# Long-run loads, an on-chip permute, four PSUM pairs at the start and weight sums spread over batch 1, in a fused ReLU²-attention and ReGLU kernel

## The chip, the cores and the metric

The kernel runs on one core of a Trainium2 chip. The metric is the device time of one execution in microseconds (us). The profile shows five engines: PE (TensorE; its weight loads are listed as PEld), DVE (VectorE), ACT (ScalarE), POOL (GpSimd) and SP (SyncE). SyncE and GpSimd mostly issue DMAs here.

## The reference, cut to what matters

```python
# q, k, v: (8, 12, 448, 64)   w_gate, w_val: (768, 1536)   w_out: (1536, 768)
scores = q @ k.transpose(0, 1, 3, 2) / sqrt(64)
attn   = maximum(scores, 0) ** 2 / 448
x      = (attn @ v) as rows: (8*448, 768)            # 3584 tokens
out    = (maximum(x @ w_gate, 0) * (x @ w_val)) @ w_out
```

The attention needs Q and K with the head dimension on the partitions, so both must be transposed on the way in. One unit of attention is a *quad*: four heads of one batch, so three quads per batch and 24 in all. From the second pair of batches on, the gate/value product uses a Strassen scheme with seven products in place of eight; it needs sums of weight blocks. The output product uses it for every pair.

## The kernel before: the parts that matter

The kernel records operations, and a small planner in the same file gives each of them a place in its engine's instruction order, from assumed durations. At run time each engine executes its list strictly in that order. An instruction that waits holds up everything behind it on its engine (SyncE's timeline below shows eight stores that go out only at 165.79 us, behind transposes).

TensorE's results go to PSUM, which the kernel divides into banks. Two pairs of banks serve attention, four single banks the feed-forward part:

```python
PAIRS = [0, 2]
SINGLES = [7, 6, 5, 4]
```

Batches 0 and 1 are loaded in long runs and transposed on TensorE. For batches 2 to 7 the load itself interleaves heads (runs of one 64-element row, one descriptor for each: 896 descriptors per DMA), and five crossbar transposes per quad (DMAs that transpose what they move), issued by SyncE, put Q and K into `qkT`:

```python
def load_qk(b, g):                       # branch for b >= 2
    st.raw_buf = Buf(r_raw)              # one buffer only (N_RAW = 1)
    for j in range(2):
        hs = slice(4*g + 2*j, 4*g + 2*j + 2)
        src = lambda x: x[b, hs].rearrange("h (p t) d -> p t h d", t=NT)
        st.qk_ops += [dma_in(lambda j=j: st.raw()[64:128, j], src(k), 896, 0.9, ...),
                      dma_in(lambda j=j: st.raw()[0:64, j],   src(q), 896, 0.9)]

def transpose_dma(b, g):
    def emit():
        nc.sync.dma_start_transpose(out=qkT[:, 0]..., in_=raw[0:64]...)        # Q, one DMA
        for j in range(2):
            for o, t0, t1 in ((0, 0, NC + 1), (1, NC + 1, NT)):
                nc.sync.dma_start_transpose(out=kT[:, o:NT:2], in_=raw[64:128, j, t0:t1]...)  # K, four
    op = Op({"SP": (0.2, 0.2)}, emit, deps=st.qk_ops, alloc=[st.qt_buf], reads=[st.raw_buf])
    op.land = 5.0
```

The weight sums of the gate/value product are twelve VectorE subtractions of 128 x 1536. All of them wait for batch 1's whole gate/value product, because three of them overwrite `wv`:

```python
T_ops = make_T([quads[(1, g)].done for g in range(NQ)] + [o for o, _ in ffn])
```

The loads of `w_out` stand in GpSimd's list behind the quads of batch 2, and so behind the wait for the single raw buffer.

## Time and profile before

463.98 us, the median of 3 runs (463.94 to 465.17). The profiled execution has a span of 464.7 us.

The stages below are cut at the first TensorE matmul of each kind: gate/value product (GV) of batches 0 and 1, output product (OUT) and Strassen gate/value product (ST) of each pair of batches. Attention of later batches runs between those matmuls.

| stage | starts at, us | length, us |
|---|---|---|
| attention of batch 0 | 0 | 43.5 |
| GV, batches 0 and 1 | 43.5 | 87.1 |
| OUT, pair 0 | 130.6 | 52.2 |
| ST, pair 1 | 182.8 | 70.6 |
| OUT, pair 1 | 253.4 | 36.6 |
| ST and OUT, pair 2 | 290.0 | 94.6 |
| ST and OUT, pair 3 (no attention left) | 384.6 | 80.1 |

The table of busy time by stretch, cut at these stages, shows where TensorE is not busy. The columns are the stretch and its length, the busy time of each engine with its instruction count, the granted TensorE clock (1.00 is full), the share of the DMA engines, and GB/s.

```profile
core 0: us, PE busy (x) PEld busy (x) DVE busy (x) ACT busy (x) POOL busy (x), PEclk, DMA share, GB/s
0.00:43.49 43.49, 28.00 (x245) 14.21 (x245) 23.89 (x36) 22.16 (x25) 26.43 (x43) 0.85 1.28 179
43.49:130.59 87.10, 80.61 (x514) 34.37 (x513) 61.66 (x91) 42.78 (x58) 31.79 (x34) 0.96 1.06 106
130.59:182.77 52.18, 42.29 (x248) 19.10 (x247) 35.55 (x63) 24.83 (x35) 19.15 (x20) 0.84 0.83 99
182.77:253.41 70.64, 65.52 (x382) 28.30 (x381) 57.49 (x102) 39.28 (x59) 27.94 (x29) 0.95 0.88 101
253.41:290.03 36.62, 32.14 (x215) 15.99 (x213) 28.89 (x56) 14.65 (x23) 13.15 (x15) 1.00 0.90 116
...
384.63:464.70 80.07, 73.02 (x404) 39.21 (x401) 44.36 (x84) 26.50 (x51) 0.00 (x0) 0.99 0.18 43
```

The pace of batch 0 can be read from ScalarE's timeline: the copy of each finished quad into `xT` (columns: start, duration, engine, line, operation and shape, and in brackets the idle time before it and what ended it).

```profile
21.54 0.91 ACT L508 CAST xT<-ps 128x896 bf16<-128x896 f32 x1 [2.25 <-PE ps L493]
31.84 0.91 ACT L508 CAST xT<-ps 128x896 bf16<-128x896 f32 x1 [2.25 <-PE ps L493]
42.10 0.91 ACT L508 CAST xT<-ps 128x896 bf16<-128x896 f32 x1 [2.25 <-PE ps L493]
```

One quad takes 10.3 us, though no engine has that much work for it. The list of waits (who waited, for whom: total, times, longest) names the two chains of the middle part: GpSimd's raw loads wait for the transposes that still read the only raw buffer, and VectorE waits 10.6 us for a `w_out` load that was issued late for that reason; TensorE waits 5.8 us behind VectorE at the same place.

```profile
POOL raw L288 <- DMA qkT<-raw: 126.7, 19, 16.1
DVE woT L583 <- DMA wo<-in_moe_w_out_dram: 10.6, 1, 10.6
PE ps L544 <- DVE hT L554: 5.8, 1, 5.8
```

SyncE's timeline shows the stores standing behind transposes. The transpose at 159.02 waited for its load, the four after it take 5.35 us to issue, and eight stores go out only then:

```profile
159.02 1.23 SPq L414 DMA_TRANSPOSE qkT<-raw  x1
160.34 5.35 SPq L419 DMA_TRANSPOSE qkT<-raw  x4
165.79 5.32 SPq L717 DMA_DIRECT2D out_dram<-o  x8
```

### The profile page before, as it was taken

How to read it: one execution, taken by the hardware profiler on the slowest of the kernel's cores; microseconds unless marked ns; L12 is line 12 of the kernel's file. 1: busy time of each engine (PE TensorE's matmuls, PEld its weight loads, DVE VectorE, ACT ScalarE, POOL GpSimd, SP SyncE). 2: the span in 40 equal slices, each digit the busy share in tenths (PEclk: the TensorE clock that was granted, in tenths of full speed). 3: DMA queues.
4: the chain of work that ended last, by engine and by line, in shares of the span. 5: the costliest groups of instructions: out<-in, count | busy, mean ns of one | idle time of the engine just before them, and what ended most of it. 6: DMA issues, size and time to landing. Idle time of an engine off the chain costs nothing.

```text
span 464.7 us, 7076 instructions
## 1 busy us (share of the span) xinstructions
PE 415.1 (89%) x2580; PEld 195.2 (42%) x2580; DVE 332.8 (72%) x576; ACT 221.9 (48%) x329; POOL 134.9 (29%) x154
## 2 busy tenths in 40 slices
PE   4768999968988948799999978999999999999994
PEld 2333444423433413244444443444444555555552
DVE  3665877709798833788979967988889686666561
ACT  2564555553574522456555434665654634444221
POOL 7745150605533353145333442253200000000000
PEclk9977999997997968799999999999999999999999
DMA  9999989999857996998669898996721332000144
GB/s 128 196 198 198 151 70 100 108 147 79 82 59 87 122 132 92 128 155 70 74 82 90 85 118 147 167 83 68 72 27 27 76 86 52 1 0 2 34 103 102
DMA packets 138659, 44.13 MB, mean 95 GB/s; under 512 B 103808, under 2 KB 138624, under 8 KB 138624
## 3 DMA queue, kind: packets, MB, share of 16 engines
q0 software_dynamic: 94528, 24.39, 54.5%
q1 hardware_dynamic: 44096, 19.29, 20.9%
q8 instruction: 20, 0.33, 0.3%
q14 instruction: 15, 0.12, 0.1%
HBM read 48.76 MB, written 11.01 MB: 129 GB/s over the span
## 4 chain that ended last, share of the span: by engine, by line
PE 71%; DMA 9%; DVE 7%; SPq 4%; ACT 4%; issue 3%; POOL 1%; DVEq 0%; POOLq 0%; ACTq 0%
PE ps L643 29%; PE ps L744 17%; PE ps L544 8%; PE ps L493 6%; PE ps L451 6%; DMA wo<-in_moe_w_out_dram 4%; SPq L419 3%; DMA out_dram<-o 3%; ACT at L465 3%; PE ps L384 2%; DVE at L467 1%; DMA qkT<-raw 1%; DVE at L470 1%; PE ps L455 1%; PE ps L485 1%
## 5 line engine op out<-in xcount | busy, mean ns | idle before, releaser
L465 ACT ACTIVATE at<-ps 128x896 bf16<-128x896 f32 x117 | 104.4, 918 | 69.2 <-PE ps L451 55.3
L470 DVE TENSOR_TENSOR at<-at 128x896 bf16<-128x896 bf16 x168 | 99.7, 618 | 13.5 <-ACT at L465 13.4
L592 ACT COPY f<-ps 128x448 f32<-128x448 f32 x105 | 55.8, 533 | 66.4 <-PE ps L643 64.5
L288 POOL DMA_DIRECT2D raw<-in_k_dram x36 | 46.2, 1284 | 141.0 <-DMA qkT<-raw 126.7
L467 DVE TENSOR_SCALAR at<-ps 128x896 bf16<-128x896 f32 x51 | 55.3, 1085 | 6.9 <-PE ps L451 6.7
L288 POOL DMA_DIRECT2D raw<-in_q_dram x36 | 59.7, 1662 | 0.3 <-DMA wv<-in_moe_w_val_dram 0.3
L643 PE MATMUL ps<-xT,gvT 128*128 128x448 bf16 x216 | 53.3, 356 | 2.6 <-DVE o L734 2.5
L643 PE MATMUL ps<-sx,wv 128*128 128x448 bf16 x216 | 52.8, 353 | 1.7 <-DVE g L662 1.1
L451 PE MATMUL ps<-qkT 64*128 64x448 bf16 x288 | 45.5, 379 | 9.8 <-ACT at L465 7.1
L643 PE MATMUL ps<-xT,wg 128*128 128x448 bf16 x216 | 52.8, 356 | 0.5 <-DVE g L700 0.5
L288 POOL DMA_DIRECT2D vv<-in_v_dram x44 | 36.4, 1044 | 47.5 <-PE ps L493 40.4
L643 PEld LDWEIGHTS <-gvT 128*128 128x128 bf16 x324 | 31.1, 98 | 37.1 <-issue 9.9
L734 DVE SCALAR_TENSOR_TENSOR o<-ps,f 128x384 f32<-128x384 f32 x40 | 22.0, 554 | 31.1 <-DMA out_dram<-o 16.0
L744 PE MATMUL ps<-wo,hT 128*128 128x384 bf16 x240 | 43.8, 326 | 0.2 <-DVE hT L666 0.2
L744 PEld LDWEIGHTS <-sh 128*128 128x128 bf16 x288 | 27.9, 101 | 36.2 <-issue 10.8
L744 PEld LDWEIGHTS <-hT 128*128 128x128 bf16 x312 | 30.1, 99 | 24.6 <-issue 5.8
L744 PE MATMUL ps<-woT,sh 128*128 128x384 bf16 x144 | 30.1, 359 | 8.4 <-DVE sh L781 8.3
L544 PE MATMUL ps<-xT,wv 128*128 128x448 bf16 x144 | 32.3, 362 | 5.8 <-DVE hT L554 5.8
L493 PE MATMUL ps<-at,vv 128*64 128x448 bf16 x264 | 33.2, 393 | 0.0
L544 PE MATMUL ps<-xT,wg 128*128 128x448 bf16 x144 | 32.6, 364 | 0.0
L594 ACT ACTIVATE f<-ps 128x384 f32<-128x384 f32 x40 | 19.6, 491 | 27.2 <-PE ps L744 26.0
L508 ACT CAST xT<-ps 128x896 bf16<-128x896 f32 x24 | 21.7, 905 | 19.4 <-PE ps L493 19.4
(56 smaller groups left out, 442.1 us busy)
## 6 DMA issues: line engine op xcount, KB each, us to landing
out_dram<-o SPq DMA_DIRECT2D x112, 96.0 KB, 2.9
vv<-in_v_dram POOLq DMA_DIRECT2D x44, 128.0 KB, 5.2
raw<-in_k_dram POOLq DMA_DIRECT2D x36, 112.0 KB, 3.9
raw<-in_q_dram POOLq DMA_DIRECT2D x36, 112.0 KB, 5.0
wg<-in_moe_w_gate_dram POOLq DMA_DIRECT2D x6, 384.0 KB, 11.3
wv<-in_moe_w_val_dram POOLq DMA_DIRECT2D x6, 384.0 KB, 11.2
wo<-in_moe_w_out_dram POOLq DMA_DIRECT2D x4, 576.0 KB, 13.2
qkT<-raw SPq DMA_TRANSPOSE x90, 3.2
```

What stands on the lines that cost most here:

```text
L288: op = Op({"POOL": (0.5 + 0.0004 * n_desc,) * 2}, lambda: nc.gpsimd.dma_start(out=dst(), in_=src), deps=deps, alloc=alloc)
L451: nc.tensor.matmul(ps[:, ps2.idx + h2, :S], lhsT=self.k_of(j, h2, c), rhs=self.q_of(j, h2), start=True, stop=True)
L465: nc.scalar.activation(at_t[at.idx], src, AF.Relu)
L467: nc.vector.tensor_scalar_max(at_t[at.idx], src, 0.0)
L470: sq = Op({"DVE": (0.535, 0.66)}, lambda: nc.vector.tensor_tensor(at_t[at.idx], at_t[at.idx], at_t[at.idx], ALU.mult), deps=[relu])
L493: nc.tensor.matmul(ps[o, ps2.idx + j, :S], lhsT=st.v_of(2 * j + h2, c), rhs=at_t[self.at[NC * j + c].idx][:, h2, :], start=False, stop=(c ...
L508: nc.scalar.copy(dst, src)
L544: nc.tensor.matmul(ps[:, pb.idx, :S], lhsT=w[:, kd, fc], rhs=xT_t[xbuf[b].idx][:, kd, :], start=(kd == 0), stop=(kd == KD - 1))
L592: nc.scalar.copy(dst, src)
L643: nc.tensor.matmul(ps[:, pb.idx, :S], lhsT=w(g)[:, fc], rhs=rhs, start=start and g == 0, stop=stop and g == KH - 1, skip_group_check=True)
L734: op = Op({"DVE": V384}, lambda: nc.vector.scalar_tensor_tensor(o_t[ob.idx], ps[:, pb.idx, :OH], float(out_scale), f_t[fb.idx][:, :OH], AL ...
L744: nc.tensor.matmul(ps[:, pb.idx, :OH], lhsT=lhs(kf), rhs=rhs(kf), start=start and kf == 0, stop=kf == FH - 1, skip_group_check=True)
```

## The change

The intent has several parts in one edit:

1. Q and K of every batch are loaded in long runs (256 descriptors per DMA). VectorE (or ScalarE) then interleaves the slots on the chip, so that each quad needs two crossbar transposes instead of five. The raw buffer is free as soon as the permute is done.
2. Batch 0 may use all four pairs of PSUM banks.
3. Weight sums: nine of the twelve are rewritten so that they no longer need the overwritten block, and can run during batch 1's gate/value product.
4. The planner prices SyncE (2.6 us per quad's transposes, 1.2 us per store), plans VectorE and ScalarE work that follows a load 4 us late, models DMAs differently, and prefers ScalarE by 0.3 us.
5. The `w_out` loads come earlier and batch 1's loads one weight chunk later. One attention buffer and one output buffer are given up for the permute's buffer.
6. Two smaller things stand in the same edit: around batch 0's last quad, the PV product (attention times V) and the next transposes come at other places in the order, and the four sums of `w_out` are rewritten so that the one that overwrites `wo` comes last.

```diff
-    PAIRS = [0, 2]
+    PAIRS, FIRST_PAIRS = [0, 2], [0, 2, 4, 6]
...
+    BIAS = 0.3
+    MARGIN = 4.0
...
+            if e in ("DVE", "ACT"):
+                r = max([r] + [d.end + self.MARGIN for d in op.deps if d.load])
...
-    N_QT, N_AT, N_X, N_F, N_G, N_O = 3, 11, 3, 5, 4, 6
-    N_RAW, N_VV = 1, 3
+    N_QT, N_AT, N_X, N_F, N_G, N_O = 3, 10, 3, 5, 4, 5
+    N_RAW, N_PERM, N_VV = 1, 1, 3
...
+        src = lambda x: x[b, hs].rearrange("h (p t) d -> p h t d", t=NT)
+        k_op = dma_in(lambda: st.raw()[64:128], src(k), 256, 1.15, alloc=[st.raw_buf] if b >= NPE else [])
+        q_op = dma_in(lambda: st.raw()[0:64], src(q), 256, 1.15)
...
+        perm = Op({"DVE": (0.25 + 0.2 * len(runs),) * 2, "ACT": (2.1, 2.2)}, None, deps=st.qk_ops, alloc=[pb], reads=[st.raw_buf])
+            for o, t0, t1 in runs:                       # two runs (even batches) or three (odd)
+                dst = perm_t[pb.idx][:, :, o:o + 2 * (t1 - t0) - 1:2]
+                ... tensor_copy(dst, src[:, :, t0:t1])
+            for a in range(2):
+                nc.sync.dma_start_transpose(out=qkT_t[st.qt_buf.idx][:, a]..., in_=perm_t[pb.idx][64 * a:64 * a + 64]...)
-        op = Op({"SP": (0.2, 0.2)}, emit, deps=st.qk_ops, alloc=[st.qt_buf], reads=[st.raw_buf])
-        op.land = 5.0
+        op = Op({"SP": (2.6, 2.6)}, emit, deps=[perm], alloc=[st.qt_buf], reads=[pb])
+        op.land = 2.8
...
-        st = Op({"SP": (0.15, 0.15)}, emit, deps=[op], reads=[ob])
+        st = Op({"SP": (1.2, 1.2)}, emit, deps=[op], reads=[ob])
...
-        if c % 2 == 0:
+        if c % 2 == 1:
             load_qk(1, c // 2)
...
-    T_ops = make_T([quads[(1, g)].done for g in range(NQ)] + [o for o, _ in ffn])
+    T_ops = make_T([quads[(1, g)].done for g in range(NQ)], [o for o, _ in ffn])   # second list: only for the three sums that overwrite wv
```

More of the change, by code (lines that the diff above doesn't have):

```diff
@@ L56 @@
     SWITCH = 0.1
+    BIAS = 0.3
+    MARGIN = 4.0
+    RESERVE = 0.0
     def __init__(self):
@@ L86, in best @@
                 s = max(r, self.t.get(e, 0.0) + self.SWITCH)
-            if c is None or s + busy < c[0]:
-                c = (s + busy, s, e)
+            f = s + busy + (self.BIAS if e == "DVE" and len(op.engs) > 1 else 0.0)
+            if c is None or f < c[0]:
+                c = (f, s, e)
         return c[1], c[2], r
@@ L98, in commit @@
         if op.load:
-            self.dmaq = max(self.dmaq, s + occ + 1.0) + op.load
-            op.end = self.dmaq + 1.0
+            self.dmaq = max(self.dmaq, s + occ + 0.3) + op.load
+            op.end = self.dmaq + 2.0
             self.landed.append(op.end)
@@ L185, in plan @@
             left = deadline(sg) - last_burst + 1 if sg is not None and deadline(sg) is not None else 0
-            gap = left_work[sg] / max(1, left) if left > 0 else 0.0
+            gap = max(0.0, left_work[sg] - P.RESERVE) / max(1, left) if left > 0 else 0.0
         else:
@@ L247 @@
     woT = pool.tile([128, 3, FH, OH], BF16, name="woT")
-    raw_t = [pool.tile([128, 2, NT, 2, D], BF16, name=f"raw{i}") for i in range(N_RAW)]
+    raw_t = [pool.tile([128, 4, NT, D], BF16, name=f"raw{i}") for i in range(N_RAW)]
+    perm_t = [pool.tile([128, 2, NT, 2, D], BF16, name=f"perm{i}") for i in range(N_PERM)]
     vv_t = [pool.tile([128, 4, NC + 2, D], BF16, name=f"vv{i}") for i in range(N_VV)]
@@ L260 @@
     r_ps = Res(8)
-    r_raw, r_vv, r_qt, r_at = Res(N_RAW), Res(N_VV), Res(N_QT), Res(N_AT)
+    r_raw, r_perm, r_vv, r_qt, r_at = Res(N_RAW), Res(N_PERM), Res(N_VV), Res(N_QT), Res(N_AT)
     r_x, r_f, r_g, r_o = Res(N_X), Res(N_F), Res(N_G), Res(N_O)
@@ L323, with slot_order, main_slot @@
     SIG = [x for c in range(NC) for x in (c, NC + 1 + c)] + [NC]
-    def q_slots(b):
-        if b < NPE:
-            return SIG if b % 2 == 0 else SIG[-1:] + SIG[:-1]
-        return list(range(NT))
-    def q_main(b):
-        return 0 if b % 2 == 0 else 1
-    def k_main(b):
-        return 1 if b < NPE and b % 2 else 0
+    def slot_order(b):
+        return SIG if b % 2 == 0 else SIG[-1:] + SIG[:-1]
+    def main_slot(b):
+        return b % 2
     def load_qk(b, g):
         st = quads[(b, g)] = Quad()
-        if b < NPE:
-            hs = slice(4 * g, 4 * g + 4)
-            st.raw_buf = None
-            st.raw = lambda: early_raw(b, g)
-            src = lambda x: x[b, hs].rearrange("h (p t) d -> p h t d", t=NT)
-            k_op = dma_in(lambda: st.raw()[64:128], src(k), 256, 1.2)
-            q_op = dma_in(lambda: st.raw()[0:64], src(q), 256, 1.2)
-            st.qk_ops = [k_op, q_op]
-        else:
-            st.raw_buf = Buf(r_raw)
-            st.raw = lambda: raw_t[st.raw_buf.idx]
-            st.qk_ops = []
-            for j in range(2):
-                hs = slice(4 * g + 2 * j, 4 * g + 2 * j + 2)
-                src = lambda x: x[b, hs].rearrange("h (p t) d -> p t h d", t=NT)
-                st.qk_ops += [dma_in(lambda j=j: st.raw()[64:128, j], src(k), 896, 0.9,
-                                     alloc=[st.raw_buf] if j == 0 else []),
-                              dma_in(lambda j=j: st.raw()[0:64, j], src(q), 896, 0.9)]
+        hs = slice(4 * g, 4 * g + 4)
+        st.raw_buf = None if b < NPE else Buf(r_raw)
+        st.raw = lambda: early_raw(b, g) if b < NPE else raw_t[st.raw_buf.idx]
+        src = lambda x: x[b, hs].rearrange("h (p t) d -> p h t d", t=NT)
+        k_op = dma_in(lambda: st.raw()[64:128], src(k), 256, 1.15, alloc=[st.raw_buf] if b >= NPE else [])
+        q_op = dma_in(lambda: st.raw()[0:64], src(q), 256, 1.15)
+        st.qk_ops = [k_op, q_op]
     def load_v(b, g):
@@ L368, in load_v @@
         st.v_of = lambda hh, c: st.vv()[:, hh, 1 + c, :]
-        v0 = dma_in(lambda: st.vv()[0:64, :, 1:NC + 2], src[:, :, 0:NC + 1], 256, 0.7,
+        v0 = dma_in(lambda: st.vv()[0:64, :, 1:NC + 2], src[:, :, 0:NC + 1], 256, 0.66,
                     alloc=[st.vv_buf] if st.vv_buf else [])
-        v1 = dma_in(lambda: st.vv()[64:128, :, 0:NC + 1], src[:, :, NC:NT], 256, 0.7)
+        v1 = dma_in(lambda: st.vv()[64:128, :, 0:NC + 1], src[:, :, NC:NT], 256, 0.66)
         st.v_ops = [v0, v1]
@@ L376, in transpose_pe @@
         st = quads[(b, g)]
-        ps2 = bank2()
+        ps2 = bank2(FIRST_PAIRS if b == 0 else PAIRS)
         def emit():
@@ L381, in emit @@
             for j in range(2):
-                for i, t in enumerate(q_slots(b)):
+                for i, t in enumerate(slot_order(b)):
                     for h2 in range(2):
@@ L410, in transpose_dma, with emit_perm @@
         st.qt_buf = Buf(r_qt)
-        def emit():
-            raw, qkT = st.raw(), qkT_t[st.qt_buf.idx]
-            nc.sync.dma_start_transpose(out=qkT[:, 0].rearrange("p j (t c) -> p (j t) c", c=P2),
-                                        in_=raw[0:64].rearrange("p j t h d -> p (j t h d)"))
-            for j in range(2):
-                kT = qkT[:, 1, j].rearrange("p (t c) -> p t c", c=P2)
-                for o, t0, t1 in ((0, 0, NC + 1), (1, NC + 1, NT)):
-                    nc.sync.dma_start_transpose(out=kT[:, o:NT:2], in_=raw[64:128, j, t0:t1].rearrange("p t h d -> p (t h d)"))
-        op = Op({"SP": (0.2, 0.2)}, emit, deps=st.qk_ops, alloc=[st.qt_buf], reads=[st.raw_buf])
-        op.land = 5.0
+        pb = Buf(r_perm)
+        m = main_slot(b)
+        runs = [(m, 0, NC + 1 - m), (1 + m, NC + 1, NT)] + ([(0, NC, NC + 1)] if m else [])
+        perm = Op({"DVE": (0.25 + 0.2 * len(runs),) * 2, "ACT": (2.1, 2.2)}, None, deps=st.qk_ops, alloc=[pb], reads=[st.raw_buf])
+        def emit_perm():
+            src = st.raw().rearrange("p (j h) t d -> p j t h d", j=2)
+            for o, t0, t1 in runs:
+                dst = perm_t[pb.idx][:, :, o:o + 2 * (t1 - t0) - 1:2]
+                if perm.eng == "ACT":
+                    nc.scalar.copy(dst, src[:, :, t0:t1])
+                else:
+                    nc.vector.tensor_copy(dst, src[:, :, t0:t1])
+        perm.emit = emit_perm
+        def emit():
+            for a in range(2):
+                nc.sync.dma_start_transpose(out=qkT_t[st.qt_buf.idx][:, a].rearrange("p j (t c) -> p (j t) c", c=P2),
+                                            in_=perm_t[pb.idx][64 * a:64 * a + 64].rearrange("p j t h d -> p (j t h d)"))
+        op = Op({"SP": (2.6, 2.6)}, emit, deps=[perm], alloc=[st.qt_buf], reads=[pb])
+        op.land = 2.8
         st.qt_ops = [op]
-        others.append(op)
+        others.extend([perm, op])
     xop, xbuf = {}, {}
@@ L437, in k_of @@
         def k_of(self, j, h2, c):
-            m = k_main(self.b)
+            m = main_slot(self.b)
             o, n = (P2 * m + 128 * c, 128) if c < NC else (0 if m else 2 * NC * P2, P2)
@@ L442, in s @@
         def s(self, i):
-            ps2 = bank2()
+            ps2 = bank2(FIRST_PAIRS if self.b == 0 else PAIRS)
             tail = i == 2 * NC
@@ L477, in pv @@
             b, g, st = self.b, self.g, self.st
-            ps2 = bank2()
+            ps2 = bank2(FIRST_PAIRS if b == 0 else PAIRS)
             def emit_tail():
@@ L559, in gv_plain, with make_T @@
         last_use[("gv", b)] = ops
-    def make_T(after):
-        res = {}
+    def make_T(after, last):
+        res = []
         for g in range(KH):
-            prev = []
-            for o, a, c in ((lambda g: gvT[:, 1, g], lambda g: wv[:, 2 * g + 1], lambda g: wv[:, 2 * g]),
-                            (lambda g: wv[:, 2 * g], lambda g: wv[:, 2 * g], lambda g: wg[:, 2 * g]),
-                            (lambda g: gvT[:, 0, g], lambda g: wv[:, 2 * g + 1], lambda g: wv[:, 2 * g]),
-                            (lambda g: gvT[:, 2, g], lambda g: wg[:, 2 * g + 1], lambda g: gvT[:, 0, g])):
-                op = Op({"DVE": (0.85, 0.97)}, lambda o=o, a=a, c=c, g=g: nc.vector.tensor_tensor(
-                    o(g), a(g), c(g), ALU.subtract), deps=after + prev)
-                others.append(op)
-                prev = [op]
-            res[g] = prev
-        return [x for p in res.values() for x in p]
+            for o, a, c, f in ((lambda g: gvT[:, 1, g], lambda g: wv[:, 2 * g + 1], lambda g: wv[:, 2 * g], ALU.subtract),
+                               (lambda g: gvT[:, 0, g], lambda g: wg[:, 2 * g], lambda g: gvT[:, 1, g], ALU.add),
+                               (lambda g: gvT[:, 2, g], lambda g: wg[:, 2 * g + 1], lambda g: gvT[:, 0, g], ALU.subtract)):
+                op = Op({"DVE": (0.85, 0.97)}, lambda o=o, a=a, c=c, f=f, g=g: nc.vector.tensor_tensor(o(g), a(g), c(g), f),
+                        deps=after + res[-1:] + list(wg_op.values()) + list(wv_op.values()))
+                others.append(op)
+                res.append(op)
+        for g in range(KH):
+            op = Op({"DVE": (0.85, 0.97)}, lambda g=g: nc.vector.tensor_tensor(wv[:, 2 * g], wv[:, 2 * g], wg[:, 2 * g], ALU.subtract),
+                    deps=res[-1:] + last)
+            others.append(op)
+            res.append(op)
+        return res
@@ L577, in make_To @@
     def make_To():
         res = []
-        for i, (o, a, c) in enumerate(((lambda: woT[:, 1], lambda: wo[:, 1, 1], lambda: wo[:, 0, 1]),
-                                       (lambda: wo[:, 0, 1], lambda: wo[:, 0, 1], lambda: wo[:, 0, 0]),
-                                       (lambda: woT[:, 0], lambda: wo[:, 1, 1], lambda: wo[:, 0, 1]),
-                                       (lambda: woT[:, 2], lambda: wo[:, 1, 0], lambda: woT[:, 0]))):
-            op = Op({"DVE": (1.25, 1.38)}, lambda o=o, a=a, c=c: nc.vector.tensor_tensor(o(), a(), c(), ALU.subtract),
+        for o, a, c, f in ((lambda: woT[:, 1], lambda: wo[:, 1, 1], lambda: wo[:, 0, 1], ALU.subtract),
+                           (lambda: woT[:, 0], lambda: wo[:, 0, 0], lambda: woT[:, 1], ALU.add),
+                           (lambda: woT[:, 2], lambda: wo[:, 1, 0], lambda: woT[:, 0], ALU.subtract),
+                           (lambda: wo[:, 0, 1], lambda: wo[:, 0, 1], lambda: wo[:, 0, 0], ALU.subtract)):
+            op = Op({"DVE": (1.25, 1.38)}, lambda o=o, a=a, c=c, f=f: nc.vector.tensor_tensor(o(), a(), c(), f),
@@ L759, in out_tail @@
         wd = list(wo_op.values())
-        slots = ((b, q_slots(b)[-1]), (b + 1, q_slots(b + 1)[0]))
+        slots = ((b, slot_order(b)[-1]), (b + 1, slot_order(b + 1)[0]))
         a0 = out_mm(lhs(0), w(0, 0), A, True, h_lo + wd, seg, [A], [hb], grp=(pr, "t"))
@@ L790, in out_strassen @@
             A, Dk, E = bank(), bank(), bank()
-            s0, s1 = [tuple((bb, q_slots(bb)[q_main(bb) + 2 * i + z]) for z in range(2)) for bb in (b, b + 1)]
+            s0, s1 = [tuple((bb, slot_order(bb)[main_slot(bb) + 2 * i + z]) for z in range(2)) for bb in (b, b + 1)]
             gr = lambda n: (pr, i, n)
@@ L816 @@
         load_gv(c)
-        if c % 2 == 0:
+        if c % 2 == 1:
             load_qk(1, c // 2)
             load_v(1, c // 2)
-    for g in range(NQ):
-        load_qk(2, g)
-        load_v(2, g)
-        if g > 0:
-            load_out(0, g - 1)
-    load_out(1, 0)
-    load_out(1, 1)
+    load_qk(2, 0)
+    load_v(2, 0)
+    for par in range(2):
+        for hf in range(2):
+            load_out(par, hf)
+        load_qk(2, 1 + par)
+        load_v(2, 1 + par)
     for b in range(3, B):
@@ L856 @@
         att.append((qd.s(2 * NC), burst))
-        PV(n - 1)
-        T(n + 1)
+        if n != NQ:
+            PV(n - 1)
+        if n != NQ - 1:
+            T(n + 1)
         burst += 1
@@ L862 @@
         att += [(qd.s(4), burst), (qd.s(5), burst)]
+        if n == NQ - 1:
+            burst += 1
+            PV(n)
+            T(n + 1)
     burst += 1
```

## The prediction

> **What bounds the kernel.** TensorE is busy 415 of 464.7 us (page, part 1). Busy time times granted clock (table by stretch) gives about 398 us of work, so some 67 us are idle or half-clock time, in three places:
> - Start, 0 to 43.5 us: batch 0's quads come every 10.3 us (timeline: score eviction at 23.50, then 33.77), though ScalarE and VectorE have only about 6.2 us of work per quad. The chain of waits alternates "scores, eviction": two PSUM pairs are too few. TensorE is cold (twelve PV matmuls take 2.45 us, later 1.32).
> - 100 to 110 us: TensorE waits 5.8 us. VectorE stands 10.6 us at the out-weight sum for a w_out load that GpSimd issued only at 85 us, because the single raw buffer waits for the transposes (126.7 us in the list of waits).
> - 130 to 200 us: twelve gate/value weight sums (0.95 us each) in a clump, then stores queued behind five crossbar DMAs per quad (1.24 us of SyncE each) that wait for loads: stores ready near 160 issue at 165.8, output buffers return late, TensorE idles 11.2 us in 160 to 200 at clock 0.79.
>
> From 200 to 250 TensorE is 99% busy, VectorE 87%; after 385 only TensorE work is left.
>
> **What the change does.**
> - Batch 0 may use four PSUM pairs. I take 7 to 7.5 us per quad (engine sums above; a cold quad of TensorE is 8.1). Gate matmuls start near 32 instead of 43.5: −11 us. Weight loads (198 GB/s there) still arrive ahead of use, by my count of bytes.
> - Raw loads of batches 2 to 7: 36+36 DMAs of 896 descriptors become 18+18 of 256; GpSimd issue falls from 1.3/1.7 to about 0.65 us each (the early loads' time), software-queue packets from 94.5k to about 39k. By itself off the critical path. The Trainium skill ("DMA: Bandwidth & Descriptors", Specifications) says transfers below 512 B do a read-modify-write; this trace shows only 103.8k packets below 512 B.
> - Transposes 90 → 36: SyncE per quad 6.6 → 2.5 us; the raw buffer is free after the permute; the w_out loads move forward. The 100–110 stall goes: −6.5 us with its clock.
> - The plan now prices SyncE, so stores no longer hide behind transposes.
> - Added: 18 permutes, all on VectorE (instruction order), 45 copies; estimate 0.7 us per quad if they run at four elements per cycle (skill, "VectorE: DVE Perf Modes", Mode 4×_2P; this trace has no such instruction), 1.1 at the squares' rate: +12 to 19 us of VectorE. 13 relus move to ScalarE: −14.
> - 130–189: my sum is TensorE 41, VectorE about 40 us; I expect 45 instead of 59: −14.
> - 250–300, 4.6 us idle: about −3. Last 80 us unchanged (both orders end with 252+150 matmuls).
>
> Sum: about 464 − 36 = 428 us.
>
> **In the profile after:** batch 0 pitch near 7.5 us; first gate matmul near 32; no wait for w_out; transposes start within a microsecond of the permute; no raw-load waits on transposes; TensorE clock near 1.0 from 50 on (skill, "TensorE: Matmul & The Clock Gate", Part 1: an idle window of about 3.4 us halves it; this trace agrees, matmuls after the 6.5 us gap at 171 take about double); VectorE share 77–80%.
>
> **What would make it wrong:** permutes near 1.5 us, or standing in VectorE's in-order queue for loads; VectorE the new bound through 110–200 (then 440); five output buffers too few; batch 0 still DMA-limited. If all gaps close: 415.
>
> 428 us, range 416 to 442; faster 0.95, same 0.04, slower 0.01.

## More of the kernel before

Timings come from three sittings. The first gave the result (before and after). Sitting A ran four experiments (a1, b1, c1, d1) on one chip. Sitting B ran the other eight on another chip, with the changed kernel repeated among them. Each sitting timed the kernel before too.

In OUT of pair 0, TensorE is idle for 10 of 52 us and has 0.84 of its clock while it works.

## The result, and the profile after

430.22 us, the median of 4 runs (428.66 to 430.43), against 463.96 us for the kernel before in the same rounds (with a fourth run of it). The ratio is 0.926, with a 95% interval of 0.923 to 0.929. Ratios in this document are the mean time of one kernel's fast runs over that of the other's of the same rounds, so they are not quite the ratio of the quoted medians. The prediction, 428 us with a range of 416 to 442, holds. Its parts do not all hold.

The same table of busy time by stretch, for the changed kernel, cut at its own stages:

```profile
0.00:29.49 29.49, 17.84 (x208) 9.57 (x209) 18.60 (x29) 19.37 (x23) 19.71 (x34) 1.00 1.24 174
29.49:120.62 91.13, 83.86 (x551) 36.13 (x548) 67.72 (x109) 53.03 (x72) 25.07 (x38) 0.94 1.13 143
120.62:156.03 35.41, 35.41 (x249) 16.93 (x247) 33.02 (x66) 23.33 (x34) 6.12 (x10) 1.00 0.89 162
156.03:222.84 66.81, 64.56 (x390) 28.42 (x389) 58.38 (x113) 44.21 (x67) 11.12 (x19) 1.00 0.76 94
222.84:253.61 30.77, 30.63 (x208) 16.01 (x206) 23.13 (x51) 15.15 (x24) 4.92 (x8) 1.00 0.72 129
...
349.08:428.60 79.52, 73.01 (x403) 39.21 (x401) 44.35 (x84) 26.53 (x51) 0.00 (x0) 0.98 0.18 43
```

| stage | before, us | after, us | difference | my prediction |
|---|---|---|---|---|
| attention of batch 0 | 43.5 | 29.5 | −14.0 | −11 |
| GV, batches 0 and 1 | 87.1 | 91.1 | +4.0 | −6.5 |
| OUT pair 0, ST and OUT pair 1 | 159.4 | 133.0 | −26.4 | −17 (14 + 3) |
| ST and OUT, pair 2 | 94.6 | 95.5 | +0.9 | 0 |
| last pair | 80.1 | 79.5 | −0.6 | 0 |
| sum | 464.7 | 428.6 | −36.1 | −34.5 named |

Three of the rows are off by 3 to 10.5 us each, and the errors cancel. A part of the first two is work that changed sides: 37 of TensorE's matmuls, 28 of them the transposes of one quad (1.71 us at 41.85 us in the kernel before), stand in front of the first gate matmul before and behind it after. Together these two rows gave −10.0 us, where I had −17.5. (The attention work is spread a little differently over the stages. The instruction order has 36 of the large score matmuls in OUT of pair 0 in both kernels, but 60 instead of 52 in the stage after it and 12 instead of 20 in the next, which is why those three stages are summed.)

The start: ScalarE's copies of the three quads are now 6 us apart, not 10.3.

```profile
16.83 0.96 ACT L511 CAST xT<-ps 128x896 bf16<-128x896 f32 x1
22.94 0.91 ACT L511 CAST xT<-ps 128x896 bf16<-128x896 f32 x1 [0.28 <-PE ps L496]
28.81 0.91 ACT L511 CAST xT<-ps 128x896 bf16<-128x896 f32 x1 [3.33 <-PE ps L496]
```

The list of waits: the 126.7 us of raw-load waits on transposes are gone, and so is the wait for `w_out`. GpSimd now waits 18.6 us for permutes. There is a new line for VectorE: it waits for the transposes to let go of the only permute buffer, and TensorE waits for VectorE's evictions of scores.

```profile
POOL raw L295 <- DVE perm L415: 18.6, 4, 9.4
DVE perm L415 <- DMA qkT<-perm: 5.2, 2, 4.7
PE ps L454 <- DVE at L470: 4.5, 4, 2.0
```

The timeline shows that new stall; with the half clock after it, it is the larger part of what keeps the GV stage long. A smaller wait comes first: TensorE stands 2.65 us until 37.76 us for the Q load of batch 1's second quad, which part 5 of the change had put one weight chunk later (f2 below removes it). VectorE's second permute stood 4.65 us, until the first transposes had landed. TensorE ran out of score evictions twice, 1.58 and 2.04 us, and then worked at about half speed until 85 us.

```profile
37.76 0.97 PE L375 MATMUL ps<-ident,gvT 128*64 128x128 bf16 x28 [2.65 <-DMA gvT<-in_q_dram]
...
69.78 0.69 DVE L415 COPY perm<-raw 128x1024 bf16<-128x1024 bf16 x2 [4.65 <-DMA qkT<-perm]
...
72.06 0.55 PE L454 MATMUL ps<-qkT 64*128 64x448 bf16 x4 [1.58 <-DVE at L470]
...
74.66 0.56 PE L454 MATMUL ps<-qkT 64*128 64x448 bf16 x2 [2.04 <-DVE at L470]
```

SyncE's timeline in OUT of pair 0: two transposes per quad, and no store stands behind a long row of them.

```profile
144.12 3.64 SPq L421 DMA_TRANSPOSE qkT<-perm  x2
147.85 7.85 SPq L722 DMA_DIRECT2D out_dram<-o  x10
155.81 3.30 SPq L421 DMA_TRANSPOSE qkT<-perm  x2
```

The permutes themselves came out as estimated. The groups by shape (count, busy us, mean ns, idle before them) sum to 14.7 us for 18 quads, 0.8 us per quad; without shapes, overlaps counted once, they are 13.2 us, 0.73 per quad.

```profile
L415 DVE COPY perm<-raw 128x768 bf16<-128x768 bf16 x27 | 8.9, 357 | 0.5 <-DMA qkT<-perm 0.5
L415 DVE COPY perm<-raw 128x1024 bf16<-128x1024 bf16 x9 | 3.8, 417 | 4.7 <-DMA qkT<-perm 4.7
L415 DVE COPY perm<-raw 128x256 bf16<-128x256 bf16 x9 | 2.0, 226 | 0.0
```

From 256 to 768 elements the copy grows by 131 ns, which is 3.9 elements per ns. That agrees with the mode of four elements per cycle in the Trainium skill ("VectorE: DVE Perf Modes", Mode 4×_2P; the page's clock is 0.96 GHz).

### The profile page after: what moved, and what is told of

It is laid out like the page before. It is cut to its first block, busy times and chain, and to the rows that moved or that the text cites. A ratio compares the mean times of both kernels' runs of the same rounds, so it can differ in the third digit from the quotient of the medians.

```text
span 428.6 us, 6975 instructions
## 1 busy us (share of the span) xinstructions
PE 399.1 (93%) x2580; PEld 190.3 (44%) x2580; DVE 324.5 (76%) x600; ACT 236.3 (55%) x350; POOL 73.1 (17%) x118
## 3 DMA queue, kind: packets, MB, share of 16 engines
q0 software_dynamic: 38656, 24.39, 43.2%
## 4 chain that ended last, share of the span: by engine, by line
PE 70%; DMA 12%; DVE 11%; issue 2%; ACT 2%; POOL 2%; SPq 1%; DVEq 0%; POOLq 0%
PE ps L648 25%; PE ps L749 22%; PE ps L547 10%; DMA gvT<-in_q_dram 7%; PE ps L496 6%; PE ps L454 5%; DMA qkT<-perm 5%; DVE at L470 2%; DVE at L473 2%; DVE g L667 1%; PE ps L458 1%; DVE perm L415 1%; DVE g L689 1%; PE ps L488 1%; DMA out_dram<-o 1%
## 5 line engine op out<-in xcount | busy, mean ns | idle before, releaser
L468 ACT ACTIVATE at<-ps 128x896 bf16<-128x896 f32 x130 | 114.8, 923 | 49.1 <-PE ps L454 36.3
L295 POOL DMA_DIRECT2D vv<-in_v_dram x44 | 27.2, 628 | 194.5 <-PE ps L496 184.7
L470 DVE TENSOR_SCALAR at<-ps 128x896 bf16<-128x896 f32 x38 | 41.2, 1084 | 15.1 <-PE ps L454 15.0
L454 PE MATMUL ps<-qkT 64*128 64x448 bf16 x288 | 42.5, 365 | 7.9 <-DVE at L470 4.5
L749 PEld LDWEIGHTS <-hT 128*128 128x128 bf16 x312 | 29.5, 98 | 23.5 <-issue 4.2
L496 PE MATMUL ps<-at,vv 128*64 128x448 bf16 x264 | 31.2, 367 | 1.6 <-DVE at L473 1.6
L648 PEld LDWEIGHTS <-wv 128*128 128x128 bf16 x216 | 20.2, 97 | 25.1 <-issue 8.4
L689 DVE CUSTOM_DVE_ANT_0 g<-ps,f 128x448 bf16<-128x448 f32 x36 | 22.3, 620 | 10.7 <-PE ps L648 10.6
L648 PEld LDWEIGHTS <-wg 128*128 128x128 bf16 x216 | 20.4, 98 | 22.1 <-issue 4.2
L599 ACT ACTIVATE f<-ps 128x384 f32<-128x384 f32 x40 | 19.7, 492 | 18.3 <-PE ps L749 16.4
## 6 DMA issues: line engine op xcount, KB each, us to landing
wg<-in_moe_w_gate_dram POOLq DMA_DIRECT2D x6, 384.0 KB, 11.3
```

The costliest lines, as they stand in the source:

```text
L295: op = Op({"POOL": (0.5 + 0.0004 * n_desc,) * 2}, lambda: nc.gpsimd.dma_start(out=dst(), in_=src), deps=deps, alloc=alloc)
L454: nc.tensor.matmul(ps[:, ps2.idx + h2, :S], lhsT=self.k_of(j, h2, c), rhs=self.q_of(j, h2), start=True, stop=True)
L468: nc.scalar.activation(at_t[at.idx], src, AF.Relu)
L470: nc.vector.tensor_scalar_max(at_t[at.idx], src, 0.0)
L496: nc.tensor.matmul(ps[o, ps2.idx + j, :S], lhsT=st.v_of(2 * j + h2, c), rhs=at_t[self.at[NC * j + c].idx][:, h2, :], start=False, stop=(c ...
L648: nc.tensor.matmul(ps[:, pb.idx, :S], lhsT=w(g)[:, fc], rhs=rhs, start=start and g == 0, stop=stop and g == KH - 1, skip_group_check=True)
```

## The experiments

All times are medians; "before" in sitting A was 460.67 us (455.51 to 462.78, seven runs) and in sitting B between 460.99 and 461.55 us as runs were added. The changed kernel was timed again under its own name in sitting B only (but see d1). All kernels but one gave correct results; that one is named.

### a1: the four PSUM pairs alone, in the kernel before

```diff
-    PAIRS = [0, 2]
+    PAIRS, FIRST_PAIRS = [0, 2], [0, 2, 4, 6]        # used by batch 0's transposes, scores and PV
```

> The kernel before with one thing of the change: batch 0 may use four PSUM pairs. In the changed kernel the first gate matmul came at 29.5 us instead of 43.5. Theory (the PSUM pairs alone are the start's gain): first gate matmul near 30 to 31 here too, and 450 to 453 us in all (-11 to -14). Rival (the start's gain needs the other load order or is swallowed later, because the wait for w_out at 100 us and the transposes depend on loads that come no earlier): first gate matmul near 30, but 457 to 463 us in all.

Measured: 459.37 us, ratio 1.000 (0.989 to 1.011): no gain that the runs can tell, though the interval leaves room for 5 us either way. The first gate matmul did come at 31.0 us in place of 43.5. But the GV stage that follows took 95.8 us in place of 87.1, OUT of pair 0 started only 3.8 us earlier than before, and the list of waits has a new line:

```profile
PE ps L451 <- DMA qkT<-raw: 9.0, 1, 9.0
```

TensorE came earlier to the scores of a later quad and waited there for its transposes. VectorE's wait for `w_out` also grew, from 10.6 to 13.9 us. The rival holds: the pairs alone bring the start forward, and the gain is given back at the next thing that depends on the loads.

### b1 and b2: the changed kernel with the old Q and K path

The Q and K path of batches 2 to 7 is put back (896-descriptor loads, no permute, five transposes), with the planner told that five transposes cost 6.6 us of SyncE; everything else of the change stays.

```diff
-        op = Op({"SP": (2.6, 2.6)}, emit, deps=[perm], alloc=[st.qt_buf], reads=[pb])
+        op = Op({"SP": (6.6, 6.6)}, emit, deps=st.qk_ops, alloc=[st.qt_buf], reads=[st.raw_buf])   # five DMAs, from raw
```

> The changed kernel with the Q and K path of the kernel before for batches 2 to 7 (896-descriptor loads, no permute, five crossbar DMAs per quad), everything else kept, the plan told that the five cost 6.6 us of SyncE. Theory (the long-run loads and two-DMA transposes carry the gain in the output stage of pair 0): 440 to 448 us (+10 to +18), the extra in 100 to 200 us, with late stores. Rival (the weight sums' new place and the priced plan carry it; the data path is off the critical path): 428 to 434 us.

b1 gave a wrong result (not-a-number): I had mixed up the row order of odd batches, so some output rows were never stored. Its time was 442.42 us in sitting A (ratio 0.964, 0.955 to 0.972).

> The run b1 repeated with its mistake mended: b1 used the wrong row order for odd batches, so that some output rows were never stored; its stores and its work were the same in number and size. Expected: correct, and the same time within noise, 0.955 to 0.97 of the kernel before.

b2 was correct, 442.18 us in sitting B (ratio 0.959, 0.953 to 0.965), 9.9 us above the changed kernel there. GpSimd's waits for the transposes are back:

```profile
POOL raw L294 <- DMA qkT<-raw: 162.7, 21, 12.8
```

TensorE was busy 23.3 of the 30 us from 130 to 160, at 0.91 of its clock; in the changed kernel it was busy 28.7 of them. So the data path is worth about 10 us when the rest of the change is there.

The loss is not where my theory put it. Against the changed kernel of the same sitting, OUT of pair 0 starts 6.4 us earlier in b2 (115.0 us, 121.4 there) and is short: 33.1 us, with 217 matmuls in it in place of 249, although stores still went out behind rows of five transposes (10 of them at 128.15 us, 14 at 144.00). The Strassen stage after it is the long one: 81.1 us with 434 matmuls, in place of 67.9 us with 390. In it TensorE waits 4.98 us for transposes, and has half its clock for a time after that:

```profile
159.10 0.93 PE L457 MATMUL ps<-qkT 64*128 64x448 bf16 x4 [4.98 <-DMA qkT<-raw]
```

Just as telling is the rest: with the old data path, the other parts together are already at 0.959.

### c1: the weight sums in one clump again

```diff
-    T_ops = make_T([quads[(1, g)].done for g in range(NQ)], [o for o, _ in ffn])
+    T_ops = make_T([quads[(1, g)].done for g in range(NQ)] + [o for o, _ in ffn])   # and the old make_T, make_To
```

> The changed kernel with the weight sums of the kernel before: all twelve gate/value sums after batch 1's gate/value stage, in one clump (nine more VectorE sums of 0.95 us in the output stage of pair 0). Theory (moving the sums is a large part of the 24 us that stage gained): 436 to 442 us (+7 to +12), all of it in 120 to 170 us. Rival (VectorE has room there once SyncE is free): 429 to 432 us.

Measured: 434.73 us (433.86 to 436.62), ratio 0.948 (0.941 to 0.956). The changed kernel was not in this sitting under its own name, but d1 below turned out to run the same instructions in the same order, at 431.69 us on the same chip, which makes the cost about 3 us. OUT of pair 0 took 41.2 us (120.89 to 162.11) in place of 35.4, but the Strassen stage after it was shorter (64.1 in place of 66.8). The clump costs something, less than the 7 to 12 us of the theory and more than the rival's nothing, and part of it is won back one stage later.

### d1: the old prices of SyncE in the planner

```diff
-        op = Op({"SP": (2.6, 2.6)}, ...);  op.land = 2.8;  st = Op({"SP": (1.2, 1.2)}, ...)
+        op = Op({"SP": (0.2, 0.2)}, ...);  op.land = 5.0;  st = Op({"SP": (0.15, 0.15)}, ...)
```

> The changed kernel planned with the old prices of SyncE (0.2 us a quad's transposes, 0.15 us a store, 5 us to land). Only the order of instructions can change. If pricing SyncE matters: 436 to 445 us with stores queued behind transposes. If two transposes per quad that wait on no load make the order harmless: 428 to 432 us.

Measured: 431.69 us (429.72 to 433.2), ratio 0.940 (0.931 to 0.949), the same as the changed kernel's ratio of 0.939 in sitting B. OUT of pair 0 took 35.4 us here as well. The trace says why: on every engine d1 runs the same operations in the same order as the changed kernel (compared by operation, line and tile, over 2,580 matmuls, 600 VectorE, 350 ScalarE and 148 SyncE instructions). The old prices change no place in the plan. So my sentence "the plan now prices SyncE, so stores no longer hide behind transposes" put the credit in the wrong place. Whether another order would do harm, with two transposes per quad, this run does not test. What it gives is the changed kernel once more, in sitting A.

### The changed kernel again, as a yardstick

> The changed kernel unchanged, as the yardstick for the runs beside it on this chip: 0.926 of the kernel before, 427 to 431 us.

Measured: 432.32 us (432.13 to 432.9), ratio 0.939 (0.933 to 0.945), a little above what I had written. On this chip the kernel before ran 1% faster than in the first sitting and the changed kernel did not. Differences below are taken against 432.32.

### a2: the changed kernel with two PSUM pairs

```diff
-    PAIRS, FIRST_PAIRS = [0, 2], [0, 2, 4, 6]
+    PAIRS, FIRST_PAIRS = [0, 2], [0, 2]
```

> The changed kernel without the four PSUM pairs of batch 0. In the kernel before, the four pairs alone brought the first gate matmul forward by 12.5 us, but a new wait of 9 us for a crossbar transpose (80 to 100 us) ate most of it. Theory (the pairs are worth their full 12 to 14 us only once the loads and transposes of batch 2 keep up, as they do here): 440 to 445 us here, first gate matmul near 42. Rival (the start's gain is eaten here too, by the stall at 70 to 80 us, which sits at a fixed time set by the loads): 431 to 436 us.

Measured: 436.28 us (434.24 to 439.86), ratio 0.948 (0.941 to 0.955): +4.0 us. The first gate matmul came at 40.6 us against 31.1, 9.5 us later, but OUT of pair 0 started only 6.9 us later. (Its profiled execution was its slowest, 438.0 us of span, against 430.5 for the changed kernel's in this sitting.) So the rival is nearer: also in the changed kernel a part of the start's gain is given back, in the GV stage.

### e1: the w_out loads late, as before

```diff
-    load_qk(2, 0); load_v(2, 0)
-    for par in range(2):
-        for hf in range(2): load_out(par, hf)
-        load_qk(2, 1 + par); load_v(2, 1 + par)
+    for g in range(NQ):
+        load_qk(2, g); load_v(2, g)
+        if g > 0: load_out(0, g - 1)
+    load_out(1, 0); load_out(1, 1)
```

> The changed kernel with the w_out loads where the kernel before had them, behind batch 2's quads. In the changed kernel the first two transposes were in flight beside two w_out loads and took 11.2 us to land (5.2 in the median); VectorE stood 4.7 us for the permute buffer they held, and TensorE lost 4.4 us and its clock from 70 to 80 us. Theory (contention with the bulk loads makes the transposes slow): first transposes land in under 6 us, no stall at 70, 423 to 427 us. Rival (the landing is slow whatever runs beside it, or the later w_out brings back a wait for it near 100 us): 428 to 433 us.

Measured: 433.14 us (428.36 to 434.37), ratio 0.939 (0.931 to 0.946): no difference. My theory that the `w_out` loads alone make the first transposes slow falls: they still took up to 9.4 us to land, and VectorE still stood 2.8 us. The timeline shows why the edit could not separate the two. The first permute frees the raw buffer. GpSimd then issued the next K and Q loads, two V loads and the first `w_out` load at 61.4 to 63.8 us, and the transposes of the same permute were issued at 61.2. The permute itself releases the traffic that runs beside its own transposes.

That this traffic slows them is not isolated by an experiment. These are the landing times in both kernels (issue to landing, us, lowest/median/highest of 2 to 6 transposes, and the GB/s of the stretch):

| kernel, stretch (us) | GB/s | landing of transposes |
|---|---|---|
| before, 120 to 140 | 74 | 2.3 / 2.4 / 3.4 |
| before, 80 to 105 (`w_out` in flight) | 119 | 9.6 / 11.5 / 13.2 |
| after, 55 to 68 | 168 | 8.1 / 9.7 / 11.2 |
| after, 92 to 105 | 92 | 9.1 / 9.2 / 9.2 |
| after, 200 to 250 | 108 | 3.5 / 3.7 / 5.2 |

The Trainium skill ("DMA: Bandwidth & Descriptors", § Issuing engines are not separate DMA queues) says that DMAs of the scalar, sync and gpsimd engines all run on the same 16 DMA engines and interleave. The mean GB/s of a stretch is a poor guide (see 92 to 105 us), so I took, from the packets in the changed kernel's trace, the share of the 16 DMA engines' time that GpSimd's queue filled while each transpose was in flight. Of the 36 transposes, the 13 that landed within 4.0 us had at most 0.06 of it beside them; the 16 that took 6.4 to 11.2 us had 0.51 to 1.01. That agrees with the page, as a correlation; in the kernel before it is weaker, with landings under 4 us at a share of up to 0.97.

### e2: a second permute buffer for one quad

```diff
-        pb = Buf(r_perm)
+        pb = Buf(r_perm) if (b, g) != (2, 1) else Buf(Res(1))      # that quad's buffer lies in sx, free until pair 1
```

> The changed kernel with a second permute buffer for the second quad of batch 2 (in the space of a tile that is free until pair 1), so that VectorE need not wait at 65 to 70 us for the first transposes to land. The landing itself stays at about 11 us. Theory (VectorE's in-order wait for the one permute buffer, not the late landing, is what stops TensorE from 70 to 80 us): VectorE idle before that permute gone, TensorE busy 9 or more of 10 us in 70 to 80, 422 to 426 us. Rival (the scores of that quad wait for the landing anyway): 427 to 431 us.

Measured: 428.15 us (427.22 to 429.4), ratio 0.930 (0.925 to 0.935), 4.2 us below the changed kernel; the four runs of each do not overlap. VectorE's idle time before the permutes on the old buffer fell from 5.6 to 1.6 us, and TensorE was busy 7.6 of the 10 us from 70 to 80 in place of 6.1, with the clock at 0.83 and then, from 80 on, at 1.00 (0.71 from 80 to 90 in the changed kernel). VectorE's in-order wait for the buffer was the larger part of the stall. What stays (0.8 and 0.5 us waits for ScalarE's evictions near 73 to 75 us) comes from an order that runs two bursts of scores together. TensorE did not reach the nine busy microseconds that I had written.

### g1: every permute executed twice

```diff
-            for o, t0, t1 in runs:
+            for o, t0, t1 in runs + runs:
```

> The changed kernel with every permute executed twice, the plan not told: 0.68 to 0.77 us more of VectorE in each of 18 quads, 13 us in all. If VectorE were the bound of the attention part: +10 to +13 us, 440 to 445. If TensorE is the bound and VectorE has slack (76% busy): +1 to +5 us, 430 to 436.

Measured: 437.09 us (434.39 to 439.69), ratio 0.949 (0.942 to 0.956): +4.8 us for 11.3 us more of VectorE (24.5 in place of 13.2). So a little less than half of an added VectorE microsecond shows in the time: VectorE is neither the bound nor free. (The doubled permute also makes everything that waits for a permute later: GpSimd's waits for permutes are 25.2 us in place of 18.6. The run does not separate the two.)

### k1: the new Q and K path alone, in the kernel before

Long-run loads, permute, two transposes, and the smaller buffer counts that make room; two PSUM pairs, the clumped sums, the old load order and all old plan constants stay.

```diff
+    perm = Op({"DVE": ..., "ACT": (2.1, 2.2)}, None, deps=st.qk_ops, alloc=[pb], reads=[st.raw_buf])
-        op = Op({"SP": (0.2, 0.2)}, emit, deps=st.qk_ops, alloc=[st.qt_buf], reads=[st.raw_buf])
+        op = Op({"SP": (0.2, 0.2)}, emit, deps=[perm], alloc=[st.qt_buf], reads=[pb])
```

> The kernel before with the new Q and K path alone: long-run loads, permute, two transposes per quad (and the one attention and one output buffer fewer that make room). Two PSUM pairs at the start, clumped sums, the old plan prices and load order are kept. Theory (the stall at 100 us and the late stores at 160 to 190 us go with the data path, so it carries more than half of the gain alone): 440 to 447 us. Rival (only the whole set works: old sums and the old plan keep the output stage of pair 0 slow): 450 to 458 us.

Measured: 473.45 us (469.94 to 476.86), ratio 1.031 (1.023 to 1.038): **slower** than the kernel before. Both numbers that I wrote down were wrong, in sign. The stall at 100 us did go (TensorE was busy 10.0 of the 10 us there), though the GV stage as a whole stayed at 87.1 us, and OUT of pair 0 was 5.3 us shorter, but both Strassen stages with attention grew, from 70.6 to 75.3 us and from 63.5 to 69.6. The group of permutes, without shapes, shows what took their place; k1 first, then the changed kernel:

```profile
L409 DVE COPY perm<-raw 128x768 bf16<-128x768 bf16 (+2 forms) x45 | 13.2, 342 | 30.0 <-DMA qkT<-perm 12.6 <-issue 10.4 <-DMA raw<-in_q_dram 7.0
```

```profile
L415 DVE COPY perm<-raw 128x768 bf16<-128x768 bf16 (+2 forms) x45 | 13.2, 343 | 5.2 <-DMA qkT<-perm 5.2
```

The same 13.2 us of copies, but VectorE stood still for 30.0 us in front of them in place of 5.2: 12.6 us for the permute buffer that transposes still read, 7.0 us for loads, and 10.4 us ("issue") for which the profile shows no wait. The old plan puts a permute into VectorE's list at the time when it thinks the load lands. When the load or the buffer is later, everything behind the permute waits, and TensorE after it. One such place from k1's timeline: the permute waits 3.79 us for a load, and TensorE then waits 4.04 us for VectorE.

```profile
184.69 0.76 DVE L409 COPY perm<-raw 128x768 bf16<-128x768 bf16 x3 [3.79 <-DMA raw<-in_q_dram]
...
187.04 1.28 PE L640 MATMUL ps<-sx,wv 128*128 128x448 bf16 x3 [4.04 <-DVE g L659]
```

In the kernel before, the wait for a load stood on SyncE, which computes nothing (though stores stood behind it). The new path moves it onto an engine that computes. In the changed kernel no permute waited for its load at all. The edit that aims at this is the planner's margin of 4 us for VectorE and ScalarE work behind a load, which is about the loads' part alone; which of the plan constants removes these waits was not run by itself and stays open.

### f2: the second permute buffer, and batch 1's loads one chunk earlier

```diff
-        if c % 2 == 1:
+        if c % 2 == 0:
             load_qk(1, c // 2)                # on top of e2
```

> The changed kernel with the second permute buffer of the earlier run and batch 1's loads one weight chunk earlier, as in the kernel before. In the changed kernel TensorE waited 2.7 us at 35 to 38 us for the Q load of batch 1's second quad. Theory (that wait is all that stands there): gone, 2 to 3 us less than with the second buffer alone, 0.915 to 0.927 of the kernel before. Rival (the same bytes come in the same time, and the gate weights come later by as much): no change, 0.928 to 0.935.

Measured: 428.94 us (426.55 to 431.42), ratio 0.933 (0.926 to 0.940): not to be told from e2. The wait at 35 to 38 us is gone (TensorE busy 10.0 of the 10 us from 30 to 40, in place of 7.35 in the changed kernel and 6.57 in e2), and OUT of pair 0 started 2.1 us earlier than in e2. The timed runs spread over 4.9 us, more than the gain looked for, so whether the 2 us are kept is open. e2 and f2 are the fastest versions found here, 1% below the changed kernel.

## Why the prediction was right, and where its parts were not

The total was right: 428 us predicted, 430.2 measured. That it came so close is luck: up to the first output matmul the gain was 7.5 us smaller than forecast, and in the three stages after it 9.4 us larger. By its steps:

- **The start.** I took 7 to 7.5 us per quad and −11 us. It was 6.0 us per quad and −14. My 7 to 7.5 lay between the other engines' 6.2 us and the 8.1 us of a cold TensorE; TensorE warmed up. Twelve PV matmuls take 2.45 us at 19 us in the kernel before, and 1.49 us at 21.4 in the changed one. The mechanism (PSUM pairs) is shown by a1 and a2: the first gate matmul moves by 12.5 and 9.5 us with that edit alone. What I did not say is that the gain is not kept by itself: a1 gained nothing that its runs can tell.
- **"The 100–110 stall goes: −6.5 us with its clock."** This step failed in the balance. The stall and the wait for `w_out` did go, but the GV stage became 4.0 us longer instead of shorter. A new stall stands at 70 to 80 us (TensorE idle for 4.4 us), with half clock after it, and the later loads of batch 1 cost 2.65 us at 35 us. I had listed "permutes … standing in VectorE's in-order queue for loads" as a risk; it was the queue, but the wait was for the permute buffer, held by two transposes that took 8.1 and 11.2 us to land there. e2 shows what this buffer costs: 4.2 us.
- **130 to 200 us.** I predicted −14, and −3 for the later idle time; these three stages gave −26.4. The mis-sized term is "TensorE 41, VectorE about 40". Measured, OUT of pair 0 is 35.4 us with TensorE busy throughout and VectorE busy for 33.0. The table of the kernel before could have told it: TensorE's 42.29 us there at 0.84 of the clock are an estimated 35.5 us of work. VectorE did not become the bound.
- **The reason for it.** Fewer transposes, free of load waits, is right for the total: b2 loses 9.9 us when the old path is put back. It is not shown for OUT of pair 0, where I had put it: with the old path back that stage still takes 33.1 us, and the loss comes in the stage after it. "The plan now prices SyncE" is wrong as a cause: d1 has the same instruction order without the prices. The spread weight sums are worth about 3 us in all and 5.8 us in OUT of pair 0 (c1, 41.2 in place of 35.4); the data path alone takes 5.3 us from that stage (k1). What gives the rest of the 16.8 us there stays open.
- **The permutes.** 0.7 us per quad was predicted, all on VectorE; 0.73 was measured. Doubling them costs 4.8 us. SyncE's part came out larger than the 2.5 us per quad that I had named: two transposes take 1.51 us each in the median to issue.
- **The profile.** GpSimd's busy time fell from 134.9 to 73.1 us and the software queue's packets from 94,528 to 38,656, as said (about 39k). VectorE's share is 76%, just under the 77 to 80% predicted. "Clock near 1.0 from 50 on" holds except for 70 to 90 us (0.71 and 0.78 in steps of 10 us). There TensorE idled for 4.4 us in all, in several gaps of which the longest took 1.58 and 2.04 us, and the clock fell. "TensorE: Matmul & The Clock Gate" (Part 1) tells of the clock falling after an idle window of about 3.4 us; the matmuls after the gap of 6.5 us before 171 us in the kernel before, at about double their time, agree with it. But the clock records here fall after less than that: at 74.1 us in the changed kernel, after 3.4 us in which TensorE was busy for 0.55 us, and at 139.4 and 166.7 us in the kernel before, after 3.4 us with 1.8 and 1.4 us of matmuls. So gaps that are each shorter than the window can cost the clock too.

What the prediction missed altogether is that the parts do not add. Undone one at a time from the changed kernel, the data path is worth 9.9 us, the pairs 4.0, the sums about 3 and the prices nothing: 17 of the 29 us that the change gives in sitting B. Done alone in the kernel before, the pairs give nothing and the data path costs 12. Each part needs the others: an earlier start is worth what the later loads and transposes can follow, and the permute is worth something only in a plan in which VectorE does not stand in front of it. The remainder lies in the combination, in the plan constants and in the small changes of order (part 6), none of which was run by itself.

## What to carry to other kernels

When a wait is moved from an idle engine to a busy in-order one, look at what stands behind it there: the same permute that is worth 10 us in one plan cost 12 us in another with the same copies. A buffer that is released earlier lets in traffic that can slow the very transfer that still needs the bandwidth, so check what the release triggers. And when a sum of terms comes out right, check the terms against the stages: here errors of +10.5 and −9.4 us cancelled.

## What the Trainium skill lacked or had wrong

- "DMA: Bandwidth & Descriptors" (§ DMA Transpose) has no duration for the issue of a crossbar transpose out of SBUF of this size on this chip. Measured: about 1.23 us of SyncE per DMA in the kernel before, the same for one that covers 64 x 1792 elements (1232 ns in the median) as for one that covers less than a third of that (1240 ns); landing after 3.5 and 2.7 us in the median. In the changed kernel each of the 36 covers 64 x 1792 elements and the median is 1508 ns, because the second of a pair mostly takes 1.6 to 2.0 us. So five transposes to two saved about half of SyncE's issue time per quad (an estimate from these medians: 6.2 to 3.0 us).
- The same page (§ Issuing engines are not separate DMA queues) says that DMAs interleave, but gives no size for the effect on small transfers beside bulk loads. Measured, as a correlation, for transposes of one size: 3.4 to 4.0 us to land with GpSimd's queue at no more than 0.06 of the DMA engines' time, 6.4 to 11.2 us with it at 0.51 to 1.01.
- "TensorE: Matmul & The Clock Gate" (Part 4) reads as if the full clock did not engage for transposes. Measured: the 28 transposes of one quad on TensorE took 1.71 us at 6.5 and 9.8 us of the changed kernel and 0.97 us at 16.4 us, once the large matmuls around them ran at full rate too.
- The same page (Part 1) says that the clock starts at half. The matmuls agree (twelve PV matmuls in 2.45 us at 19 us, 1.32 us later), but the granted clock of the kernel before's profile reads 1.00 over the first 20 us. Before the first recorded transition, the matmuls' own durations are the better witness. The page's warnings on clock records do not name this case.
